# Strassen's seven products for half of a first feed-forward layer, in six of eight batches

## The chip, the cores and the metric

The kernel runs on one core of a Trainium2 chip, as a single launch. The metric is device time in microseconds (us): the median of several runs of the whole program. A core has five engines that matter here, each with its own in-order queue of instructions: TensorE (PE in the profile; its weight loads are listed apart as PEld), VectorE (DVE), ScalarE (ACT), GpSimd (POOL) and SyncE (SP), which issues most of the DMAs. Matmuls add up in PSUM, an on-chip memory of eight banks; all else lies in SBUF.

## The reference

```python
def _attn_ref(q, k, v, g_q, g_k):            # (8, 12, 448, 64): batch, heads, seq, head_dim
    q_n, k_n = rmsnorm(q, g_q), rmsnorm(k, g_k)
    scores = np.matmul(q_n, k_n.transpose(0, 1, 3, 2)) / np.sqrt(64)
    attn = np.exp(scores - scores.max(-1, keepdims=True))
    attn = attn / (attn.sum(-1, keepdims=True) + 1e-9)
    return np.matmul(attn, v)

def _moe_ref(x, w_in, w_out):                # x: (3584, 768), w_in: (768, 2048), w_out: (2048, 768)
    h = x @ w_in
    return gelu_tanh(h) @ w_out
```

The attention output of the 12 heads is laid side by side to make x (8 batches of 448 tokens, 768 columns), and x goes through two dense layers with a tanh-GELU between them. d_ff is 2048, which the kernel sees as 16 blocks of 128.

## The kernel before, in words

**Stages.** Batch after batch (loop at L1009) the kernel alternates two stages. The first-layer stage of batch b multiplies win by x of that batch and applies the GELU into the tile g. The attention stage of batch b+1 (`attention`, L584) then runs scores, exponentials, row sums and the product with v of the next batch, and fills the gaps on TensorE with the second layer (wout times g) of an earlier batch, cut into steps by the generator `quartered` (L475, one step is four matmuls; written "r" in the order string). Batch 0 has its own code. After the first layer of batch 7, `final` (L728) does the last 512 tokens of the second layer with Strassen's seven products in place of eight, in two halves of 128 tokens each.

**TensorE.** In the steady stages the 128x128 array is used as four 64x64 quadrants. The two row halves r hold two halves of the contraction, the two column halves a hold two halves of the output block. Four matmuls, one for each quadrant, run side by side; four such matmuls are called a quad below. Both row halves must add into the same PSUM bank, but not at the same time, so the work goes in two turns: in turn 0 row half r writes bank r, in turn 1 it writes bank 1-r, and `follows` (L468) makes TensorE wait for its own matmul at a change of turn. `mm1_turn` (L523) does one turn for a pair of d_ff blocks: six quads of 448 columns over the six contraction chunks c. There are eight pairs of blocks, so a first-layer stage of a batch from 1 on has 8 pairs x 2 turns x 6 chunks x 4 = 384 matmuls of 448 columns, and eight GELUs on ScalarE (L543).

**PSUM.** The eight banks are four tiles of two banks, in the list `rounds`; `pair` (L70) takes the one that is longest in use. The open second-layer tile is taken out of the list while it is filled, so the units of attention (one unit: the scores of one block of keys, "u") rotate among the other three. A unit can start only when the earlier content of its tile was read: by the exponential (L343), by a product's reader, or by an eviction of a finished second-layer tile (`evict`, L505, "E").

**Order.** The order on TensorE within a steady attention stage is written out by hand in STEADY (L571). Its first string is TensorE's: "5r u 11r uu 8r uu 8r 1r u 6r u 4r u 5r uu 6r su ..." where s is the row sums of a chunk of heads and x its product with v. Its second string is VectorE's: "A0 E0 B0 F0 G0 T0 R0 ..." where A, B, F and G add exponentials (L355 to L362), E0 evicts the first second-layer tile (L513), T, R and S make and spread reciprocals, and M writes x (`quad_x`, L418, L422). The product s of a chunk reads the result of G. What stands in the list "first" of `extra` is issued at the start of the stage, ahead of A0 on its queue.

**Side work of a first-layer stage.** A table of steps (`m1`, L1038 to L1074) issues at given places the work for later batches: GpSimd normalizes q and k of batch b+1 (L278), SyncE transposes them by DMA (L319) and loads batch b+2 (L124), ScalarE and GpSimd square them (L162, L164), VectorE sums the squares (L173) and scales kT (`gain`, L325). A 1x1 copy (`gpsimd_waits`, L874) makes GpSimd wait for VectorE.

**Batch 7.** The same table issues the sums of weights (`weight_sum`, L712, four operations of 3072 elements per partition) and of tokens (`token_sums`, L719) for the last stage.

## Time and profile before

| what | us |
|---|---|
| median of 3 runs (388.73 to 389.92) | 389.68 |
| the profiled execution's own time | 389.53 |
| its span, first to last instruction | 387.8 |
| between the two | 1.73 |
| TensorE matmul busy in the span | 379.0 |
| ScalarE busy | 276.6 |
| VectorE busy | 259.9 |
| GpSimd busy | 126.0 |

The profile is that of one execution. Its page gives busy time by engine, the chain of work that ended last, and groups of instructions with their mean duration in ns; the trace behind it answers by line, by shape and by time. Times in a timeline are us from the start of the span; an engine's next independent instruction can start a little before the one ahead is listed as ended, and a matmul's listed duration holds its way through the array, so the pace of TensorE is read from start to start.

### The profile page before, as it was taken

How to read it: one execution, taken by the hardware profiler on the slowest of the kernel's cores; microseconds unless marked ns; L12 is line 12 of the kernel's file. 1: busy time of each engine (PE TensorE's matmuls, PEld its weight loads, DVE VectorE, ACT ScalarE, POOL GpSimd, SP SyncE). 2: the span in 40 equal slices, each digit the busy share in tenths (PEclk: the TensorE clock that was granted, in tenths of full speed). 3: DMA queues.
4: the chain of work that ended last, by engine and by line, in shares of the span. 5: the costliest groups of instructions: out<-in, count | busy, mean ns of one | idle time of the engine just before them, and what ended most of it. 6: DMA issues, size and time to landing. Idle time of an engine off the chain costs nothing.

```text
span 387.8 us, 17506 instructions
## 1 busy us (share of the span) xinstructions
PE 379.0 (98%) x8020; PEld 294.2 (76%) x8020; DVE 259.9 (67%) x394; ACT 276.6 (71%) x348; POOL 126.0 (33%) x109
## 2 busy tenths in 40 slices
PE   8899999999999999999999999999999999999995
PEld 5565586679888788877888778877888778887653
DVE  5998949984896259835589156963588503895743
ACT  6995599677994689757996589946897449953400
POOL 5996504448105440083102740064400810000000
PEclk9999999999999999999999999999999999999999
DMA  8999999979914992369822995159823630220033
GB/s 274 318 232 210 210 227 230 263 176 181 222 44 99 258 199 55 85 139 224 176 73 64 181 257 110 45 111 235 111 61 82 109 59 19 69 64 5 2 79 83
DMA packets 65085, 54.66 MB, mean 141 GB/s; under 512 B 37748, under 2 KB 61172, under 8 KB 65012
## 3 DMA queue, kind: packets, MB, share of 16 engines
q1 hardware_dynamic: 54576, 41.43, 44.5%
q0 software_dynamic: 10128, 11.80, 18.4%
q8 instruction: 62, 1.02, 1.0%
q10 hardware_dynamic: 308, 0.33, 0.3%
q14 instruction: 11, 0.09, 0.1%
HBM read 45.61 MB, written 11.01 MB: 146 GB/s over the span
## 4 chain that ended last, share of the span: by engine, by line
PE 92%; ACT 5%; DMA 1%; issue 1%; DVE 0%; POOL 0%
PE t L537 33%; PE t L495 32%; PE t L387 9%; PE t L335 8%; PE t L754 5%; ACT ex L343 4%; PE t L556 4%; DMA rawq<-in_q_dram 1%; PE h L436 1%; PE tp L296 1%; PE o L387 0%; POOL nrmq L278 0%; DVE ss L173 0%; ACT sq L162 0%; PE os L387 0%
## 5 line engine op out<-in xcount | busy, mean ns | idle before, releaser
L343 ACT ACTIVATE ex<-t,shift 128x896 bf16<-128x896 f32 x168 | 156.1, 1012 | 3.0 <-PE t L335 2.6
L495 PE MATMUL t<-wout,g 64*64 64x384 bf16 (+1 forms) x3456 | 152.0, 305 | 0.0
L495 PEld LDWEIGHTS <-g 64*64 64x64 bf16 x3456 | 115.4, 107 | 17.6 <-issue 0.2
L537 PE MATMUL t<-xT,win 64*64 64x448 bf16 x2688 | 128.7, 349 | 0.0
L537 PEld LDWEIGHTS <-win 64*64 64x64 bf16 x2688 | 98.0, 107 | 29.2
L543 ACT ACTIVATE g<-t 128x896 bf16<-128x896 f32 x56 | 50.5, 915 | 56.8 <-PE t L537 56.7
L173 DVE TENSOR_REDUCE ss<-sq 128x14 f32<-128x896 f32 (+3 forms) x45 | 44.3, 998 | 49.4 <-ACT sq L162 47.0
L335 PE MATMUL t<-qT,kT 64*64 64x448 bf16 x672 | 59.9, 351 | 1.5 <-ACT ex L343 0.6
L876 POOL COPY mark<-es 1x1 bf16<-1x1 bf16 x7 | 1.2, 177 | 134.8 <-DVE es L362 126.4
L355 DVE TENSOR_TENSOR es<-ex 128x1792 bf16<-128x1792 bf16 x21 | 22.3, 1061 | 28.9 <-ACT ex L343 28.9
L278 POOL TENSOR_TENSOR nrmq<-rawq,rinv 128x896 bf16<-128x896 f32 (+1 forms) x21 | 34.8, 1658 | 19.5 <-ACT rinv L205 10.5
L278 POOL TENSOR_TENSOR nrmk<-rawk,rinv 128x896 bf16<-128x896 f32 (+1 forms) x21 | 34.6, 1647 | 0.0
L387 PE MATMUL t<-ex,vb 64*64 64x448 bf16 x588 | 32.4, 350 | 0.5 <-issue 0.5
L335 PEld LDWEIGHTS <-kT 64*64 64x64 bf16 x672 | 26.2, 106 | 8.0 <-issue 1.9
L397 DVE STREAM_TRANSPOSE st<-t 128x448 f32<-128x448 f32 x42 | 24.7, 627 | 9.6 <-PE t L387 9.6
L387 PEld LDWEIGHTS <-vb 64*64 64x64 bf16 x672 | 23.2, 107 | 8.6 <-issue 2.1
L409 DVE STREAM_TRANSPOSE rb<-rc 128x896 f32<-128x896 f32 (+1 forms) x25 | 26.7, 1068 | 0.3
L422 DVE TENSOR_TENSOR xT<-t,rb 128x896 bf16<-128x896 f32 x21 | 22.8, 1086 | 0.9 <-PE t L387 0.2
L513 ACT COPY osb<-t 128x768 f32<-128x768 f32 (+1 forms) x18 | 12.6, 701 | 14.0 <-PE t L495 14.0
L358 DVE TENSOR_TENSOR es<-es,ex 128x1792 bf16<-128x1792 bf16 x21 | 22.3, 1062 | 0.0
L164 POOL TENSOR_TENSOR sq<-rawq 128x896 f32<-128x896 f32 (+1 forms) x9 | 13.6, 1510 | 24.3 <-DVE ss L173 11.6
L325 DVE TENSOR_SCALAR kT<-kT,gcols 128x896 bf16<-128x896 bf16 x19 | 12.1, 639 | 11.2 <-DMA kT<-nrmk 11.2
(122 smaller groups left out, 322.5 us busy)
## 6 DMA issues: line engine op xcount, KB each, us to landing
rawq<-in_q_dram SPq DMA_DIRECT2D x22, 448.0 KB, 4.6
rawk<-in_k_dram SPq DMA_DIRECT2D x22, 448.0 KB, 6.3
out_dram<-osb SPq DMA_DIRECT2D x36, 192.0 KB, 2.8
vb<-in_v_dram POOLq DMA_DIRECT2D x6, 672.0 KB, 8.1
out_dram<-osb SPq DMA_DIRECT2D x38, 96.0 KB, 2.2
win<-in_moe_w_in_dram POOLq DMA_DIRECT2D x8, 384.0 KB, 10.4
wout<-in_moe_w_out_dram POOLq DMA_DIRECT2D x3, 768.0 KB, 17.2
vb<-in_v_dram POOLq DMA_DIRECT2D x2, 448.0 KB, 15.2
```

Source lines behind the costliest of these rows:

```text
L173: nc.vector.reduce_sum(sss[b][:, seat(b, c), "qk".index(n), hs, ts], squares(b, c, n, hs, ts), axis=AX.X)
L278: eng.tensor_mul(nrms[n, b, c][:, ts].rearrange("p t a d -> p a t d"), raws[n, b, c][:, :, ts], root[:, :, ts].to_broadcast([P, 2, m, D]),)
L335: nc.tensor.matmul(sc[r * R:(r + 1) * R, a, :S], kT[rs, c, t, r], qT[b][rs, c, :, r], start=True, stop=True,)
L343: nc.scalar.activation(exs[b, c][:, t], scs.pop((b, c, t))[:, :, :S], AF.Exp, scale=scale, bias=shift)
L355: nc.vector.tensor_add(es, ex[:, :2], ex[:, 2:4])
L387: nc.tensor.matmul(o[r][a * D:(a + 1) * D], vb[b % 2][rs, 2 * c + a, i] if what else ones[rs], es[i][rs, a], start=(i == 0), stop=(i == n ...
L397: nc.vector.transpose(st[:, r].rearrange("p a b -> p (a b)"), o[r])
L409: nc.vector.transpose(oas["rb"][:, rs].rearrange("p r s -> p (r s)"), rc.to_broadcast([128, (rs.stop - rs.start) * m, 32]),)
L422: nc.vector.tensor_mul(xT[b][:, 2 * c:2 * c + 2], oas["o", c, 1][:, :, :S], oas["rb"])
L495: mm = nc.tensor.matmul(o[a * R:(a + 1) * R, bank, :hi - lo], g[rs, f, at:at + R], wout[rs, f, lo:hi], start=(n == 0), stop=(n == len(step ...
L537: mm = nc.tensor.matmul(h[a * R:(a + 1) * R, j, :S], win[rs, c, at:at + R], xT[b][rs, c], start=begin and c == cs[0], stop=end and c == cs ...
L543: nc.scalar.activation(g[:, 2 * i:2 * i + 2, (b % 2) * S:(b % 2 + 1) * S], h[:, :, :S], AF.Gelu_apprx_tanh,)
```

## The change

**First layer of batches 2 to 7.** Eight of the 16 d_ff blocks (0 to 3 and 8 to 11) are computed by Strassen's seven products instead of eight. The weights are cut by d_ff (blocks 0 to 3 against 8 to 11) and by contraction (even against odd chunks); x is cut by tokens (two times 224) and by contraction. One product in one turn is `half`: 24 matmuls of 224 columns, six quads. The class `Seven` holds three PSUM tiles X, Y and Z. Products accumulate in them: X takes products 1, 6, 7 and 4 one after the other, Y takes 2, Z takes 5 and 3. In between ScalarE copies X to SBUF three times (`keep`, float32, 896 elements per partition), and VectorE adds a kept X to Y, a kept X to Z, and the other kept X to Z again (three additions of 896). Four GELUs read the results, each for four blocks and 224 tokens. The other eight blocks ("lone" pairs 2, 3, 6, 7) stay with `mm1_turn`, in parts of three chunks put between the products. `rest` is the written-out order.

**Sums.** `in_sums` makes the weight sums once: four VectorE operations on 3 x 512 bfloat16 elements per partition, put last in "first" of the attention stage of batch 2; one of them overwrites a quarter of the used part of win. `x_sums` makes four sums of 3 x 224 elements at the start of each of the six first-layer stages.

**Side work.** From batch 2 on the table has new places: the four squares of batch b+2, chunk 0, come first on ScalarE; GpSimd waits for `x_sums` between the first and the second chunk that it normalizes; one square of chunk 1 goes from ScalarE to GpSimd; loads, transposes, totals and gains have other steps.

**Memory.** x has one buffer instead of two, rb shares the buffer of st, and one weight sum of the last stage lies in two raw tiles.

**Last stage.** `weight_sum(1)` moves from the first-layer stage of batch 7 into `final`, behind the last token sums. The second row of each half is stored as whole rows, one DMA on SyncE's queue and one on ScalarE's, instead of two halves with two DMAs each on SyncE's.

```diff
-    xp = ctx.enter_context(tc.tile_pool(name="xp", bufs=2))
+    xp = ctx.enter_context(tc.tile_pool(name="xp", bufs=1))
...
-            oas["rb"] = stp.tile([128, 2, S], F32, tag="rb", name="rb")
+            oas["rb"] = stp.tile([128, 2, S], F32, tag="st", name="rb")
...
+    def in_sums():
+        a11, a21, a12, a22 = wv[:, 0, :, fs1], wv[:, 0, :, fs2], wv[:, 1, :, fs1], wv[:, 1, :, fs2]
+        nc.vector.tensor_sub(wx[:, 1], a21, a11)
+        nc.vector.tensor_add(wx[:, 0], wx[:, 1], a22)
+        nc.vector.tensor_sub(wx[:, 2], a12, wx[:, 0])
+        nc.vector.tensor_add(a21, a21, a22)
...
+        def half(self, i, name, turn, ms=range(NCH)):
...
+            if before != turn:
+                follows(mm)
...
+            for n in range(2):
+                for m in ms:
+                    for r in range(2):
+                        bank, rs = (r + turn) % 2, slice(r * D, (r + 1) * D)
+                        for a in range(2):
+                            at = (bank * 2 + n) * 128 + a * R
+                            mm = nc.tensor.matmul(
+                                t[a * R:(a + 1) * R, bank, n * QS:(n + 1) * QS],
+                                self.lhs[i][rs, m, at:at + R], self.rhs[i][rs, m],
...
+        def early(self):
+            two = range(NCH - 1)
+            for turn in range(2):
+                mm1_turn(self.b, LONE[0], turn, early, begin=not turn)
+                self.half(1, "X", turn, two)
+                self.half(2, "Y", turn, two)
+        def rest(self, steps):
...
+            self.x_sums()
+            side(0)
+            half(1, "X", 1, one)
+            mm1_turn(b, LONE[0], 1, late)
+            half(2, "Y", 1, one)
+            half(1, "X", 0, one)
+            self.keep(0)
+            mm1_turn(b, LONE[0], 0, late, end=True)
+            half(2, "Y", 0, one)
+            add(self.of("Y"), self.of("Y"), self.snaps[0])
+            self.gelu(self.of("Y"), 0, 0)
+            side(1)
+            lone(1, 0, 0, begin=True)
+            half(6, "X", 0)
+            side(2)
+            lone(1, 0, 1)
+            half(5, "Z", 0)
+            half(6, "X", 1)
+            self.keep(1)
+            side(5)
+            half(5, "Z", 1)
+            lone(1, 1, 0)
+            side(8)
+            half(7, "X", 1)
+            rounds.append(rounds.pop(0))
+            lone(2, 0, 0, begin=True)
+            half(7, "X", 0)
+            self.keep(0)
+            add(self.snaps[0], self.of("Z"), self.snaps[0])
+            lone(1, 1, 1, end=True)
+            self.gelu(self.snaps[0], 1, 1)
+            side(11)
+            lone(2, 0, 1)
+            half(4, "X", 0)
+            half(3, "Z", 1)
+            half(4, "X", 1)
+            self.gelu(self.of("X"), 1, 0)
+            side(15)
+            lone(3, 0, 0, begin=True)
+            half(3, "Z", 0)
+            add(self.of("Z"), self.of("Z"), self.snaps[1])
+            self.gelu(self.of("Z"), 0, 1)
+            side(17)
+            lone(3, 0, 1)
+            lone(2, 1, 0)
+            lone(2, 1, 1, end=True)
+            lone(3, 1, 0)
+            lone(3, 1, 1, end=True)
...
+        if b > 1:
+            sevens[b] = Seven(b)
+            sevens[b].early()
...
         token_sums(slice(NJ - 2, NJ))
+        weight_sum(1)
...
-            put_out(t, 1, last)
             add(c2[:, first], product(4, t), c2[:, first])
-            put_out(t, 1, first)
+            put_out(t, 1, slice(0, d_model), (nc.sync, nc.scalar))
...
+            extra += [("first", lambda: gain(2, 2)), ("first", in_sums)]
+        elif b + 1 < B:
+            m1 += [(0, lambda: gpsimd_waits(ess[b, NCH - 1][:1, 0, 0, :1])),
+                   (0, lambda: normed_both(b + 1, 0, nc.gpsimd)),
+                   (0, lambda: gpsimd_waits(sevens[b].xs[:1, 3, 0, :1])),
+                   (0, lambda: normed_both(b + 1, 1, nc.gpsimd)),
+                   (0, lambda: normed_both(b + 1, 2, nc.gpsimd)),
+                   (2, lambda: transposed(b + 1, 0)), (8, lambda: transposed(b + 1, 1)),
+                   (11, lambda: transposed(b + 1, 2))]
...
+                m1 += [(5, lambda n=n: total(b + 2, 0, n)) for n in "qk"]
+                m1 += [(15, lambda a=a: squared(b + 2, 1, "q", a)) for a in range(2)]
+                m1.append((15, lambda: square(b + 2, 1, "k", nc.gpsimd)))
+                m1 += [(17, lambda n=n: total(b + 2, 1, n)) for n in "qk"]
+                for n in "qk":
+                    m1.append((17, lambda n=n: square(b + 2, 2, n, nc.gpsimd)))
+                    extra.append(("first", lambda n=n: total(b + 2, 2, n)))
+            m1 += [(5, lambda: gain(b + 1, 0)), (17, lambda: gain(b + 1, 1))]
             extra.append(("first", lambda: gain(b + 1, 2)))
+        else:
+            m1 += [(5, sums_homes), (5, lambda: weight_sum(3)), (5, lambda: weight_sum(2)),
+                   (11, lambda: weight_sum(4)), (17, lambda: token_sums(slice(2, 6))),
+                   (17, lambda: token_sums(slice(0, 2)))]
```

More of the change, by code (lines that the diff above doesn't have):

```diff
@@ L568 @@
+    sevens = {}
     early, late = range(HP - 2), range(HP - 2, HP)
@@ L716, in weight_sum @@
         x, y = {3: (b12, b22), 2: (b11, sw[3]), 4: (b21, sw[2]), 1: (b12, b11)}[i]
+        if i == 4:
+            m = NJ // 2
+            for n, t in enumerate(sw[4]):
+                js = slice(n * m, (n + 1) * m)
+                nc.vector.tensor_sub(t, x[:, js], y[:, js])
+            return
         nc.vector.tensor_sub(sw[i], x, y)
@@ L1037 @@
                     (f"a{at}", lambda n=n: total(2, 0, n))]
[L1038 removed]
+        elif b == 1:
             m1.append((0, lambda: gpsimd_waits(ess[b, NCH - 1][:1, 0, 0, :1])))
[L1041 to L1055 removed]
@@ L1056 @@
-        if 0 < b and b + 2 < B:
-            m1.append((4, lambda: loads(b + 2, 1)))
-            if b > 1:
-                m1.append((8, lambda: loads(b + 2, 2)))
+            halves = [(n, slice(a, a + 1)) for n in "qk" for a in range(2)]
+            m1 += [(0, lambda n=n, hs=hs: square(2, 1, n, nc.gpsimd, hs)) for n, hs in halves]
+            m1 += [(0, lambda n=n, hs=hs: total(2, 1, n, hs)) for n, hs in halves]
+            m1 += [(0, lambda n=n: total(2, 2, n)) for n in "qk"]
+            m1.append((0, lambda: rsqrt_last(2, slice(1, NCH))))
@@ L1068 @@
-        if 0 < b and b + 1 < B:
-            extra.append(("first", lambda: gain(b + 1, 2)))
-        if b + 1 == B:
-            m1.append((4, sums_homes))
-            m1 += [(f, lambda i=i: weight_sum(i)) for f, i in ((4, 3), (6, 2), (8, 4), (10, 1))]
-            m1 += [(f, lambda js=js: token_sums(js))
-                   for f, js in ((7, slice(0, 4)), (11, slice(4, 6)))]
+                m1.append((13, lambda n=n: square(3, 2, n, nc.gpsimd)))
+                extra.append(("first", lambda n=n: total(3, 2, n)))
@@ L1075 @@
         m1 = plan(*m1)
-        for f in range(nf // 2 if b == 0 else nf):
+        if b > 1:
+            sevens[b].rest(m1)
+        for f in range((nf // 2, nf)[b] if b < 2 else 0):
             i, part = f // 4 * 2, f % 4
```

116 lines of the change are left out of this document (87 added, 29 removed).

## The prediction, made before the changed kernel was run

> **What bounds the kernel now.** I read the page's busy shares first, then the chain of work that ended last, then who waited on TensorE, then the timelines of one first-layer stage and of the start of one attention stage.
>
> ```profile
> span 387.8 us, 17506 instructions
> PE 379.0 (98%) x8020; PEld 294.2 (76%) x8020; DVE 259.9 (67%) x394; ACT 276.6 (71%) x348; POOL 126.0 (33%) x109
> ...
> PE 92%; ACT 5%; DMA 1%; issue 1%; DVE 0%; POOL 0%
> ```
>
> TensorE is the bound: it carries 92% of the chain. In its waits the longest total is 0.8 us, at the start (L1133 is the launch); behind it comes one of 0.6 us:
>
> ```profile
> PE o L269 <- PEq L1133: 0.8, 1, 0.8
> PE t L335 <- ACT ex L343: 0.6, 2, 0.3
> ```
>
> So from batch 1 on nothing holds TensorE up. A matmul less is time less, and a wait added to TensorE is time more, since no later wait is there to absorb it. The rest is a balance of the two.
>
> **Matmuls saved.** The chain shows a whole first-layer stage, and stretches of second-layer matmuls that are only 192 columns wide:
>
> ```profile
> 211.07 18.16 PE t L537 x384
> ...
> 249.78 2.13 PE t L495 x84
> ...
> 253.24 0.91 PE t L495 x44
> ```
>
> A stage is 96 quads of 448 columns in 18.16 us: 0.189 us a quad. Eleven quads of 192 columns (the last row) take 0.91 us: 0.083. On the line through the two, a quad of 224 columns takes 0.096 us. The eight blocks cost 48 quads of 448 now, 9.08 us; the seven products cost 7 x 2 turns x 6 = 84 quads of 224, 8.06 us. That is 1.02 us less in each of six stages, 6.1 us in all, if nothing waits. A stage would last 17.14 us.
>
> Here the Trainium skill speaks against the change. Its page "TensorE: Matmul & The Clock Gate", section "Wait — 56ns, not 53.3ns?", has starts of matmuls never closer than about 25 ns. By it a quad would last 0.100 us and the stage 17.5 us, 0.34 us of the 1.02 us lost. The eleven quads of 192 run at 0.91/44 = 20.7 ns a matmul, below that floor, so I go by the row; but that burst is short, and the rivals return to it.
>
> **Waits added within a stage.** Products that add in one tile X are separated by a copy to SBUF on ScalarE, and Z by an addition on VectorE. Prices, from the groups by shape (the copy of 896 elements is extended from 384 and 768, the addition of 896, from PSUM and SBUF, is taken as the like product that writes x):
>
> ```profile
> L543 ACT ACTIVATE g<-t 128x896 bf16<-128x896 f32 x56 | 50.5, 915 | 56.8 <-PE t L537 56.7
> ...
> L422 DVE TENSOR_TENSOR xT<-t,rb 128x896 bf16<-128x896 f32 x21 | 22.8, 1086 | 0.9 <-PE t L387 0.2
> ...
> L513 ACT COPY osb<-t 128x768 f32<-128x768 f32 x12 | 9.7, 812 | 0.0
> ...
> L513 ACT COPY osb<-t 128x384 f32<-128x384 f32 x6 | 2.9, 478 | 14.0 <-PE t L495 14.0
> ```
>
> The copy: 0.812 + 128 x (0.812 - 0.478)/384 = 0.92 us. The addition: 1.09 us. Then the lags between engines, from three timelines: TensorE to ScalarE, ScalarE to VectorE and TensorE to VectorE.
>
> ```profile
> 210.87 0.95 PE L537 MATMUL t<-xT,win 64*64 64x448 bf16 x16
> ```
> ```profile
> 215.28 1.73 ACT L543 ACTIVATE g<-t 128x896 bf16<-128x896 f32 x2 [3.14 <-PE t L537]
> ```
> ```profile
> 364.81 0.92 ACT L543 ACTIVATE g<-t 128x896 bf16<-128x896 f32 x1 [0.22 <-PE t L537]
> 365.76 0.42 DVE L723 TENSOR_TENSOR vb<-g 128x512 bf16<-128x512 bf16 x1 [1.66 <-ACT g L543]
> ...
> 371.21 1.46 PE L754 MATMUL t<-tw,vb 128*128 128x384 bf16 x8
> ...
> 371.41 0.56 DVE L771 TENSOR_TENSOR osb<-t,osb 128x384 f32<-128x384 f32 x1 [0.67 <-PE t L754]
> ```
>
> The first pair of blocks is done after 22 quads, 4.16 us behind 210.87, at 215.03; its GELU starts at 215.28: 0.25 us. A GELU that ends at 365.73 starts VectorE at 365.76: 0.03. A product that gives way to the next at 371.21 starts VectorE at 371.41: 0.20. From ScalarE or VectorE back to TensorE I take 0.05 (a row for it comes below).
>
> Now the written order. Between the last matmul of `half(7, X, 0)` and the first of `half(3, Z, 1)` TensorE has two lone parts of three quads (0.567 each) and `half(4, X, 0)` (0.575): 1.71 us of work. `half(3, Z, 1)` must wait until the addition has read Z, and the addition until the copy is made: 0.25 + 0.92 + 0.03 + 1.09 + 0.05 = 2.34 us. TensorE stands for 0.63 us. Three times a copy of X alone stands between (in front of `half(6, X, 0)`, `half(7, X, 1)` and `half(4, X, 0)`): 0.25 + 0.92 + 0.05 = 1.22 against 1.14 us of other work, 0.08 each; the third lies within the 0.63. Sum 0.79 us a stage: the stage lasts 17.9 us, and six stages give 6 x (18.16 - 17.93) = 1.4 us, not 6.1. Bounds: nothing waited, 6.1; copy and addition 0.1 us longer each, 0.5 us less a stage, 1.6 us worse than before in all. I take 1.4, since each term has a row.
>
> What is queued behind TensorE's wait for Z is the rest of the stage. What else lies on the other queues is free at the time:
>
> ```profile
> 210.86 1.28 ACT L675 ACT_TABLE_LOAD   x1
> ```
> ```profile
> 212.27 1.09 DVE L422 TENSOR_TENSOR xT<-t,rb 128x896 bf16<-128x896 f32 x1
> ```
> ```profile
> 212.64 1.68 POOL L278 TENSOR_TENSOR nrmk<-rawk,rinv 128x896 bf16<-128x896 f32 x1
> ```
> ```profile
> L162 ACT ACTIVATE sq<-rawq 128x448 f32<-128x448 f32 x22 | 11.9, 570 | 0.4 <-DMA rawq<-in_q_dram 0.4
> ```
>
> The four squares ahead of the first copy (0.57 us each) fill ScalarE's hole behind the table load, from 212.14 to 214.4; that copy is due 4.25 us behind the stage's start, at 215.1. `x_sums` follows VectorE's x at 213.36. Its four sums are 672 elements each; the row of 512 above took 0.42, so I take 0.5. It is needed 5.2 us behind the start, at 216.1, by its second sum; even if GpSimd's operation held it up until 214.32 it would be in time. GpSimd's new wait for `x_sums` costs it 1 to 2 us (214.32 to about 216); behind it lie two chunks to normalize, and on SyncE's queue their transposes and the loads of batch b+2, all wanted only at steps 15 and 17 or in the next attention stage. The two totals (1.08 each) and the gain (0.44) at step 5, from 217.2, end before the late addition at 222.5. At the end, the addition on Z and two GELUs (1.09, 0.9, 0.9) fit beside the last five parts (2.84 us), so the last GELU starts as late behind the last matmul as now, and the exponentials too.
>
> **The weight sums.** They are issued once, on VectorE, ahead of A0 in the attention stage of batch 2. That stage before, VectorE and then TensorE:
>
> ```profile
> 99.55 0.44 DVE L325 TENSOR_SCALAR kT<-kT,gcols 128x896 bf16<-128x896 bf16 x1
> 100.25 1.09 DVE L355 TENSOR_TENSOR es<-ex 128x1792 bf16<-128x1792 bf16 x1 [0.27 <-ACT ex L343]
> 101.26 0.95 DVE L513 COPY osb<-t 128x768 f32<-128x768 f32 x1
> ...
> 103.97 0.63 DVE L362 TENSOR_TENSOR es<-es,ex 128x896 bf16<-128x896 bf16 x1
> ```
> ```profile
> 102.27 0.47 PE L335 MATMUL t<-qT,kT 64*64 64x448 bf16 x4
> ...
> 104.65 0.45 PE L387 MATMUL t<-es,ones 64*64 64x448 bf16 x4
> ```
>
> E0 empties the PSUM tile at 102.21, and the unit that takes this tile, the eighth (u7), starts at 102.27; G0 ends at 104.60 and the row sums s0 that read it start at 104.65. This is the lag of 0.05, and it says that VectorE has no slack here at all: A0 later by so much is TensorE later by so much. In front of A0 VectorE is idle for 0.27 us only. The price of the four sums lies between two rows:
>
> ```profile
> L717 DVE TENSOR_TENSOR tw<-wout,tw 128x3072 bf16<-128x3072 bf16 x2 | 3.5, 1755 | 0.0
> ...
> L724 DVE TENSOR_TENSOR kT<-vb,g 128x1024 bf16<-128x1024 bf16 x1 | 0.7, 693 | 0.0
> ```
>
> 1536 elements: 0.69 + 512 x 1.06/2048 = 0.96 us; where the next does not need the one before, it starts 0.08 early, as 101.26 against 100.25 + 1.09 shows; four of them 3.6 us. A0 starts 3.6 - 0.27 = 3.3 us late, and u7 with it. Behind u7 everything on TensorE queues, and no wait further on gives it back. Bounds: 0.57 ns an element, as the longer row has it, gives 3.5 - 0.27 = 3.2 and with all overlap 3.0; 0.68, as the shorter, gives 3.9. I take 3.3.
>
> **The rest.** `weight_sum(1)` (1.75 us) in `final` ends some 6 us behind the first-layer stage and is needed by the seventh product of 1.30 us, at 7.8; the PSUM tile that it keeps the addition of the second product from emptying is needed at 6.5, so nothing, or 0.3 us if I am that far out. rb in st's buffer, and x in one: their users follow each other on VectorE or lie a stage apart; nothing.
>
> At the very end SyncE's issues are the queue:
>
> ```profile
> 382.39 1.11 SPq L456 DMA_DIRECT2D out_dram<-osb  x2
> ...
> 384.44 0.56 SPq L456 DMA_DIRECT2D out_dram<-osb  x1
> ```
> ```profile
> out_dram<-osb SPq DMA_DIRECT2D x36, 192.0 KB, 2.8
> ...
> out_dram<-osb SPq DMA_DIRECT2D x38, 96.0 KB, 2.2
> ```
>
> With two issues less the last one goes out at about 383.55 instead of 384.44; but twice 192 KB now leave at 382.4 at once, and what used to leave from 381.1 is late by 1.3 us. Between -0.9 and +0.4 I take -0.3.
>
> Sum against the profiled run's own 389.53: -1.4 + 3.3 - 0.3 = +1.6, so **391.1 us**; the median of the runs shown is 389.68, 0.15 above that run, which is within what I can tell.
>
> **Rivals.**
>
> *The waits for X and Z are hidden.* If TensorE were let into Z before copy and addition are both through, most of the 6.1 us comes: at best 389.5 - 6.1 + 3.3 - 0.3 = 386.4. Against it stands a row for each term. 5%.
>
> *The weight sums are hidden,* because A0 is late for other reasons, or u7's tile is free before: 389.5 - 1.4 - 0.3 = 387.8. Against it: 0.27 us of idle and 0.06 between E0 and u7. 8%.
>
> *VectorE is late for A0 in the later stages too* (slower). In the following stages A0 still has room:
>
> ```profile
> 230.23 1.08 DVE L173 TENSOR_REDUCE ss<-sq 128x14 f32<-128x896 f32 x1 [0.58 <-POOL sq L164]
> 231.24 0.44 DVE L325 TENSOR_SCALAR kT<-kT,gcols 128x896 bf16<-128x896 bf16 x1
> 235.24 1.09 DVE L355 TENSOR_TENSOR es<-ex 128x1792 bf16<-128x1792 bf16 x1 [3.56 <-ACT ex L343]
> ```
>
> This one A0 waited 3.56 us for its exponentials. GpSimd's last squares, which the totals ahead of A0 need, start only when VectorE has freed their buffers, behind the addition on Z: I make them end some 1.7 us later than now, and a gain caught behind a GpSimd operation can add 1.6 us, as this one shows, beside which GpSimd was running:
>
> ```profile
> 308.03 2.01 DVE L325 TENSOR_SCALAR kT<-kT,gcols 128x896 bf16<-128x896 bf16 x1 [4.13 <-DMA kT<-nrmk]
> ```
> ```profile
> 308.11 1.68 POOL L278 TENSOR_TENSOR nrmq<-rawq,rinv 128x896 bf16<-128x896 f32 x1
> ```
>
> It decides from 3.56 us on; each microsecond beyond, in four stages, is 4 us. With half a microsecond to one: 393 to 395. 17%.
>
> *Matmuls of 224 columns can't be issued at that pace for long* (slower). They must start every 24 ns, in parts of 24. The longest fast stretch of the rows above is the 84 matmuls in 2.13 us (five quads of 384 columns and 16 of 192), 25.4 ns each. If that is the limit, 336 matmuls a stage lose 336 x 1.4 ns = 0.47 us, six stages 2.8 us: 393.9. Against it: the 44 at 20.7 ns, and the pace of the whole stage, 528 matmuls in 17.1 us, 32 ns each. 8%. By the 25 ns of the skill's rule above it would be 6 x 0.34 = 2.0 us, 393.1.
>
> *The clock drops.* The wait at u7 leaves TensorE idle for 3.3 us. Every slice of the page shows nine tenths or more, with no idle stretch of that length to read from:
>
> ```profile
> PEclk9999999999999999999999999999999999999999
> ```
>
> If the clock came back at half for as long as the wait, the kernel would lose 3.3/2 us more: 392.8. 5%. The same page of the Trainium skill (section "What's actually happening") says that one idle window of about 3.4 us, free-running, halves the clock; 3.3 us would just not fill one, and no run here shows it.
>
> **How the numbers follow.** The forecast has 57%; its own range is 390.0 to 392.3, from the bounds of the Z wait (half of them on each side) and the tail. The two faster rivals have 13%, the three slower ones 30%. About 0.3% (1.2 us) is what a measurement of this kernel can tell from no change. The lower 40% of the forecast, 23%, lies within it of 389.68, with 1% more for half-hidden sums: faster 12%, same 24%, slower 64%. The range of eight in ten leaves out the fully hidden waits, half of the hidden sums and the dearer half of the VectorE rival: 388.2 to 394.0.
>
> **What would show it.** Right: in the profile after, 17.9 us for a first-layer stage, with a TensorE wait of 0.6 us on the addition's line in each of six stages and about 0.1 on the copy's; one wait of about 3.3 us at L335 for E0's copy in the stage of batch 2; A0 elsewhere still waiting for the exponentials. Wrong: first-layer matmuls of 224 columns at more than 0.1 us a quad; TensorE waits at other attention stages; a granted clock below 1; no TensorE wait at u7.

## The result and the profile after

| | before | changed kernel |
|---|---|---|
| median, us | 389.21 (388.55 to 389.92, 4 runs) | 399.11 (396.4 to 400.26, 4 runs) |
| ratio | | 1.0239 [1.0208, 1.027] |
| the profiled execution's own time | 389.53 | 396.4 |
| its span | 387.8 | 394.6 |

The changed kernel is slower: by 2.4% in the ratio above, by 9.9 us between the medians. Forecast were 391.1 us and a range up to 394.0; the side was right, the size was not. A second series of the same kernel (r_after, below) gave 398.33. The profiled execution, at 396.4, is the fastest of its four; what the others had on top is taken up with the clock.

The first and second part of the page of the changed kernel, and its chain by engine:

```profile
span 394.6 us, 19289 instructions
PE 376.3 (95%) x8884; PEld 301.5 (76%) x8884; DVE 299.2 (76%) x441; ACT 290.2 (74%) x358; POOL 134.3 (34%) x118
...
PE 79%; DVE 8%; ACT 6%; issue 2%; DMA 2%; POOL 1%; SPq 1%; DVEq 0%; ACTq 0%; POOLq 0%
```

TensorE is busy for 2.7 us less than before (376.3 against 379.0), but the span is 6.8 us longer: 9.5 us more in which it stands. Its instructions are 864 matmuls and 864 weight loads more. Its waits, longest total first:

```profile
PE t L537 <- issue: 3.8, 3, 1.7
PE t L335 <- DVE osb L513: 2.6, 1, 2.6
PE t L627 <- DVE xs L696: 1.8, 5, 0.4
PE t L627 <- issue: 1.0, 1, 1.0
```

Two of the four are the prediction's own: u7 behind E0 (L513), and product 3 behind the addition on Z (L696). The other two are "issue": time in which TensorE waited for nothing that the profile names, in the middle of a first-layer stage. The chain of waits says where. A stage runs from its first L537 to the first L495 behind it:

```profile
123.87 0.76 PE t L537 x16
...
138.95 2.27 PE t L537 x47
141.22 1.67 issue
...
143.80 0.81 PE t L495 x20
...
170.66 0.76 PE t L537 x16
171.42 0.77 PE t L627 x32
172.19 0.76 PE t L537 x16
172.94 0.96 PE t L627 x40
177.00 1.73 PE t L627 x72
...
181.17 0.92 ACT xs L641
182.11 1.10 DVE xs L696
183.26 1.34 PE t L627 x48
...
188.63 0.81 PE t L495 x20
...
215.64 0.76 PE t L537 x16
...
227.74 1.04 issue
...
233.25 1.72 issue
...
236.27 0.80 PE t L495 x17
...
263.17 0.76 PE t L537 x16
...
281.90 0.81 PE t L495 x20
...
308.86 0.76 PE t L537 x16
...
326.78 0.81 PE t L495 x20
```

The stages of batches 2 to 6 last 19.93, 17.97, 20.63, 18.73 and 17.92 us, and that of batch 7, read the same way, 17.97. Where nothing is called "issue", a stage has the 17.93 us that were forecast. In the stages of batches 2, 4 and 5 it is 2.0, 2.7 and 0.8 us longer: 5.5 us in all, 4.8 of them listed as idle on issue. The attention stage of batch 2 is the other loss; VectorE there, and TensorE's unit u7:

```profile
99.41 0.95 DVE L577 TENSOR_TENSOR wx<-win 128x1536 bf16<-128x1536 bf16 x1
...
102.26 0.95 DVE L580 TENSOR_TENSOR win<-win 128x1536 bf16<-128x1536 bf16 x1
103.13 1.08 DVE L355 TENSOR_TENSOR es<-ex 128x1792 bf16<-128x1792 bf16 x1
104.13 0.95 DVE L513 COPY osb<-t 128x768 f32<-128x768 f32 x1
```
```profile
105.13 0.38 PE L335 MATMUL t<-qT,kT 64*64 64x448 bf16 x4 [2.64 <-DVE osb L513]
```

The four sums, 0.95 us each as forecast, put A0 from 100.25 to 103.13 and u7 from 102.27 to 105.13. So the 6.8 us by which the span grew are: 2.8 in the attention stage of batch 2, 5.5 in the stages with idle on issue, less 1.3 for six stages (6 x 18.16 - 6 x 17.95), less about 0.2 in the later attention stages and at the end.

### The profile page after: what moved, and what is told of

It reads as the page before. It is cut to its first block, busy times and chain, and to the rows that moved or that the text cites. A ratio compares the mean times of both kernels' runs of the same rounds, so it can differ in the third digit from the quotient of the medians.

```text
span 394.6 us, 19289 instructions
## 1 busy us (share of the span) xinstructions
PE 376.3 (95%) x8884; PEld 301.5 (76%) x8884; DVE 299.2 (76%) x441; ACT 290.2 (74%) x358; POOL 134.3 (34%) x118
## 3 DMA queue, kind: packets, MB, share of 16 engines
q8 instruction: 69, 1.13, 1.2%
## 4 chain that ended last, share of the span: by engine, by line
PE 79%; DVE 8%; ACT 6%; issue 2%; DMA 2%; POOL 1%; SPq 1%; DVEq 0%; ACTq 0%; POOLq 0%
PE t L495 29%; PE t L537 13%; PE t L627 12%; PE t L387 8%; PE t L335 7%; PE t L920 5%; ACT ex L343 4%; PE t L556 4%; DVE ss L173 2%; DMA kT<-nrmk 2%; DVE xs L696 1%; ACT xs L641 1%; DMA rawq<-in_q_dram 1%; POOL nrmq L278 1%; DVE st L397 1%
## 5 line engine op out<-in xcount | busy, mean ns | idle before, releaser
L495 PE MATMUL t<-wout,g 64*64 64x384 bf16 (+1 forms) x3456 | 153.1, 305 | 0.0
L495 PEld LDWEIGHTS <-g 64*64 64x64 bf16 x3456 | 117.5, 107 | 16.8 <-issue 0.5
L537 PE MATMUL t<-xT,win 64*64 64x448 bf16 x1536 | 87.3, 349 | 3.9 <-issue 3.8
L537 PEld LDWEIGHTS <-win 64*64 64x64 bf16 x1536 | 54.7, 107 | 15.1 <-issue 5.7
L335 PE MATMUL t<-qT,kT 64*64 64x448 bf16 x672 | 61.0, 351 | 4.0 <-DVE osb L513 2.6
L173 DVE TENSOR_REDUCE ss<-sq 128x14 f32<-128x896 f32 (+3 forms) x45 | 43.4, 994 | 8.0 <-ACT sq L162 5.6
L543 ACT ACTIVATE g<-t 128x896 bf16<-128x896 f32 x32 | 29.2, 917 | 9.5 <-PE t L537 9.4
L627 PEld LDWEIGHTS <-win 64*64 64x64 bf16 x1152 | 31.5, 107 | 5.4 <-issue 2.5
L641 ACT COPY xs<-t 128x896 f32<-128x896 f32 x18 | 16.3, 907 | 26.1 <-PE t L627 22.5
L335 PEld LDWEIGHTS <-kT 64*64 64x64 bf16 x672 | 27.4, 106 | 10.7 <-issue 4.3
L387 PE MATMUL t<-ex,vb 64*64 64x448 bf16 x588 | 32.4, 350 | 0.2 <-issue 0.2
L387 PEld LDWEIGHTS <-vb 64*64 64x64 bf16 x672 | 22.7, 107 | 8.9 <-issue 1.6
L627 PEld LDWEIGHTS <-wx 64*64 64x64 bf16 x864 | 23.3, 106 | 6.0 <-issue 2.9
L645 ACT ACTIVATE g<-t 128x896 bf16<-128x896 f32 x18 | 16.5, 917 | 10.7 <-DVE t L708 5.1
```

The costliest lines, as they stand in the source:

```text
L173: nc.vector.reduce_sum(sss[b][:, seat(b, c), "qk".index(n), hs, ts], squares(b, c, n, hs, ts), axis=AX.X)
L335: nc.tensor.matmul(sc[r * R:(r + 1) * R, a, :S], kT[rs, c, t, r], qT[b][rs, c, :, r], start=True, stop=True,)
L387: nc.tensor.matmul(o[r][a * D:(a + 1) * D], vb[b % 2][rs, 2 * c + a, i] if what else ones[rs], es[i][rs, a], start=(i == 0), stop=(i == n ...
L495: mm = nc.tensor.matmul(o[a * R:(a + 1) * R, bank, :hi - lo], g[rs, f, at:at + R], wout[rs, f, lo:hi], start=(n == 0), stop=(n == len(step ...
L537: mm = nc.tensor.matmul(h[a * R:(a + 1) * R, j, :S], win[rs, c, at:at + R], xT[b][rs, c], start=begin and c == cs[0], stop=end and c == cs ...
L543: nc.scalar.activation(g[:, 2 * i:2 * i + 2, (b % 2) * S:(b % 2 + 1) * S], h[:, :, :S], AF.Gelu_apprx_tanh,)
```

## The experiments

The question was what the idle on issue is. **Theory:** TensorE's instructions come from memory by DMA in blocks of 16 KB, and a block comes late where the loads of q and k fill the DMA engines; the change raises a stage from 768 instructions (384 matmuls, as many weight loads) to 1056, so blocks are used up faster. **Rival 1:** matmuls of 224 columns in quadrants can't be issued at that pace, loads or not. **Rival 2:** it is a wait for X, Y or Z that the profile doesn't name.

**The same matmuls on the whole array (e1_full).** One matmul of 128x128 weights instead of four of 64x64, in the seven products alone:

```diff
-                    for r in range(2):
-                        bank, rs = (r + turn) % 2, slice(r * D, (r + 1) * D)
-                        for a in range(2):
-                            at = (bank * 2 + n) * 128 + a * R
-                            mm = nc.tensor.matmul(
-                                t[a * R:(a + 1) * R, bank, n * QS:(n + 1) * QS],
-                                self.lhs[i][rs, m, at:at + R], self.rhs[i][rs, m],
...
+                    at = (turn * 2 + n) * 128
+                    nc.tensor.matmul(
+                        t[:, turn, n * QS:(n + 1) * QS],
+                        self.lhs[i][:, m, at:at + 128], self.rhs[i][:, m],
```

> The changed kernel, but the seven products use the whole 128x128 array: 84 matmuls of 224 columns a stage in place of 336, of the same 0.096 us each as a quad; all else stays. TensorE then has 552 matmuls' instructions in a first-layer stage, not 1056 counted with the weight loads' pairs but half of that. Theory 'fetch' (TensorE runs out of instructions, since a block of 16 KB lasts 4.2 us in the new stages and its DMA is late among the loads): the idle times put down to 'issue' in the stages of batches 2, 4 and 5 go, about 5 us, and the stage lasts 17.9 us everywhere; 391 to 392 us. Rival 'own waits' (the idle comes from something in the order of the products, such as a wait that the profile does not name): the idle stays, 396 to 399 us.

Measured: 403.48 us (402.27 to 404.1, 4 runs) against 389.45, ratio 1.0345 [1.0309, 1.038]. The idle on issue within the stages is gone, but every stage now lasts about 19.8 us. The chain of its second such stage, to be laid beside the four lines from 170.66 above:

```profile
171.99 0.76 PE t L537 x16
172.75 0.87 PE t L621 x8
173.62 0.88 PE t L537 x16
174.50 1.06 PE t L621 x10
```

The same work takes 0.87 instead of 0.77, 0.88 instead of 0.76, 1.06 instead of 0.96: each change between quadrants and whole array costs 0.10 to 0.12 us, and a stage has some twenty. The Trainium skill has this in "TensorEngine Tiling (Array Packing)", section "Key Properties": a change of tiling mode drains TensorE. The run thus fits the theory on the idle, but its time, far from the 391 to 392 of that theory, measures something else.

**No loads in those stages (e2_noloads).** The loads of chunks 1 and 2 of q and k are left out in the first-layer stages of batches 2 to 5 and chunk 0's data used again, so the outputs of those chunks are another's:

```diff
-                m1 += [(2, lambda: loads(b + 2, 1)), (8, lambda: loads(b + 2, 2))]
+                for n in "qk":
+                    for c in (1, 2):
+                        raws[n, b + 2, c] = raws[n, b + 2, 0]
```

> The changed kernel without the loads of q and k, chunks 1 and 2, in the first-layer stages of batches 2 to 5 (batches 4 to 7 use chunk 0's data again: this part of the computation is left out). TensorE's instructions are unchanged. Theory 'fetch', if the lateness of the blocks comes from the loads' traffic: no idle 'issue' over 0.3 us, 391 to 393 us. If the number of instructions alone is too much for the fetch: idle stays as in the changed kernel, 396 to 399 us. Rival 'own waits': the same 396 to 399.

Measured: 391.85 us (389.89 to 392.83, 10 runs) against 389.45, ratio 1.0053 [1.0029, 1.0077]. All six stages last 17.9 us, and no wait on issue is left in them; TensorE's two longest are

```profile
PE t L335 <- DVE osb L513: 2.6, 1, 2.6
PE t L627 <- DVE xs L696: 2.1, 6, 0.4
```

With the loads gone, some 7 us of the 9.9 are gone (by medians; the profiled run, with 5.5 us of idle, was the fastest of the changed kernel), and the matmuls are issued at the forecast pace. Rivals 1 and 2 both fall as causes by themselves.

**The count of instructions without Strassen (e3_split).** The kernel before, with the matmuls of eight blocks of batches 2 to 7 each cut into two of 224 columns: 576 matmuls a stage, no copies, no sums.

```diff
+            parts = (0, S // 2, S) if b > 1 and i in (0, 1, 4, 5) else (0, S)
+            for lo, hi in zip(parts, parts[1:]):
...
-                            h[a * R:(a + 1) * R, j, :S], win[rs, c, at:at + R], xT[b][rs, c],
+                            h[a * R:(a + 1) * R, j, lo:hi], win[rs, c, at:at + R],
+                            xT[b][rs, c, lo:hi],
```

> The kernel before, with no Strassen, but the matmuls of eight d_ff blocks in batches 2 to 7 cut in two of 224 columns: 576 matmuls a stage in place of 384, the same sums, the same order and waits. By the pace of a quad (0.096 against 0.189) a stage grows by 0.13 us, all by 0.8 us: 390. Theory 'fetch': TensorE idles on 'issue' in some of the stages that load, 2 to 5 us in all: 392 to 395. Rival 'own waits': no such idle, 390.

Measured: 400.49 us (400.26 to 405.27, 4 runs) against 389.45, ratio 1.0301 [1.0236, 1.0366]. A cut that changes no dependence costs as much as the whole change (11.0 us against 9.9 between the medians, with intervals that overlap), and more than the 392 to 395 that the theory gave. The chain of its first such stage:

```profile
120.33 11.53 PE t L539 x387
131.87 1.30 issue
133.17 4.10 PE t L539 x128
137.27 1.82 issue
139.09 3.18 PE t L539 x61
```

Here one sees the block. Between two idles lie 128 matmuls, in this stage and in the three that follow; with their weight loads that is 256 instructions. The changed kernel shows the same: from 228.78 to 233.25 its timeline holds 128 matmuls. And the size fits the row of the instruction queue in the changed kernel's profile, 69 transfers with 1.13 MB, 16 KB each: 64 bytes an instruction. The row follows TensorE's count from kernel to kernel: 62 transfers with the 8020 matmuls before, 69 with 8884, 48 with the 6184 of e6. The idle is 9.3 us in eight places (L539 on issue), none in the stages of batches 6 and 7, which load nothing. The Trainium skill, "Runtime: NRT & Kernel Launch", section "Instruction fetch mechanics", has the blocks of 16 KiB, 256 instructions, and calls the cost of passing from one to the next mostly hidden. The size agrees; that it is hidden does not, by 1.3 and 1.8 us here.

**The same cut without the loads (e8_split_noloads).** The edit of e3, and the loads left out as in e2 (the same chunks' outputs are another's):

```diff
-            m1.append((4, lambda: loads(b + 2, 1)))
...
+                for n in "qk":
+                    for c in (1, 2):
+                        raws[n, b + 2, c] = raws[n, b + 2, 0]
```

> The kernel before with the matmuls of eight d_ff blocks of each first-layer stage of batches 2 to 7 cut into two of 224 columns, and without the loads of chunks 1 and 2 of q and k in those stages of batches 2 to 5 (the data of chunk 0 is used again, so the output for those chunks is another). Theory (TensorE's instructions, fetched in blocks of 16 KB, come late where those loads fill the DMA queues): no stage idles more than 0.3 us on issue, and the time is 388 to 392 us where the same cut with its loads took 400.5. Rival (the number of instructions alone is more than TensorE can be given, loads or not): the idle of some 1.3 to 1.8 us a block stays, and the time is 398 to 402.

Measured: 390.52 us (390.27 to 391.49, 10 runs) against 389.62, ratio 1.0024 [1.0002, 1.0046], and in the chain each of its six stages is one piece, without an idle:

```profile
122.38 18.28 PE t L539 x576
```

So count alone isn't it (18.28 against 18.16), and loads alone aren't either, since the kernel before has them: it is both. The DMA queues of the changed kernel in its first Strassen stage (123.9 to 143.8), then in that of batch 6 (308.9 to 326.8), which transposes but loads no q and k:

```profile
q1 hardware_dynamic: 7056, 3.84, 98.2%
q8 instruction: 3, 0.05, 1.0%
```
```profile
q1 hardware_dynamic: 5728, 1.57, 61.9%
q8 instruction: 4, 0.07, 1.5%
```

The columns are packets, MB and share of the 16 engines. The instruction blocks are 1% of the load beside 98% of other traffic. The kernel before has nearly as full a stage (92.9%), but a block of 128 matmuls lasts it 128/384 x 18.16 = 6.1 us, and the new one 128/528 x 17.95 = 4.4.

The trace holds each transfer of the instruction queue, and so it shows the late blocks themselves. In the changed kernel's profile there are four such idles. Their transfers began at 140.44, 226.46, 232.57 and 275.55, landed 0.93 to 1.03 us later, and TensorE went on 1.3 to 1.5 us behind each landing, every time 88 to 91 matmuls past a multiple of 128. The eight idles of e3 end likewise, 1.2 to 1.5 us behind a landing. The transfers are not slow: the median of all 69 is 0.98 us. They start late. Counted from the step of TensorE into the block before (the matmul 128 earlier), those four began after 2.7 to 4.0 us, with the DMA engines full all that time; in the stage of batch 6 none began later than 0.6 us. The idle at 233.25 is one such sum: 3.8 us to the start, 0.9 for the transfer and 1.5 behind it make 6.2 us, for a block that lasts 4.5.

**Strassen from batch 3 only (e4_from3).** Batch 2 keeps its first layer as before, and the weight sums go into that stage.

```diff
-            extra += [("first", lambda: gain(2, 2)), ("first", in_sums)]
+            extra += [("first", lambda: gain(2, 2))]
+        elif b == 2:
...
+            m1 += [(9, lambda: gain(b + 1, 0)), (10, in_sums), (14, lambda: gain(b + 1, 1)),
+                   (15, last_sum)]
```

> The changed kernel, but Strassen from batch 3 on only, and the weight sums in the first-layer stage of batch 2, where VectorE has idle time: three of them at step 10, the one that overwrites win at step 15. The wait of 2.9 us at the eighth unit goes, and batch 2's own 0.2 us of gain and its idle with it. Profiled run 391 to 394 by what is left of the idle. Theory 'clock' (the spread of the changed kernel's runs, 396.4 to 400.3 at a granted clock of 0.999 to 0.991, is the clock dropping behind the 2.9 us wait): all runs at 0.998 or more and within 1.5 us of each other. Rival: the drop follows the idle on 'issue', then clocks of 0.991 to 0.996 stay.

Measured: 391.7 us (390.16 to 396.52, 10 runs) against 389.45, ratio 1.0055 [1.0028, 1.0082]. The wait at u7 is gone and the clock is 0.997 or more in every run. Leaving out the longest run, 396.52, the other nine still spread by 3.7 us, where I had expected 1.5; idle on issue is still there in the profiled one (1.2 and 0.4 us), and how late a block comes need not be the same in each run, though only one was profiled.

**The changed kernel again (r_after).** No edit.

> The changed kernel again, unaltered, beside its variants on the same chip. By the theory as it stands (a wait of 2.9 us for the weight sums, 3 to 7 us of TensorE idle on 'issue' in stages that load, 1.7 us more when the clock comes back at half behind the first wait, and 0.2 us gained in each stage) it takes 396 to 401 us, with a median near 399, and runs with a granted clock of 0.995 or less are the slower ones.

Measured: 398.33 us (396.89 to 399.66, 4 runs) against 389.02, ratio 1.0236 [1.0197, 1.0275]. The wait at u7 was 3.42 us in this profile, the idle on issue at L537 4.6.

**Another order in the last third (e5_order).** A lone part goes ahead of product 3, so that more work stands between the reads of Z:

```diff
+            side(15)
+            lone(2, 1, 0)
             half(3, "Z", 1)
             half(4, "X", 1)
             self.gelu(self.of("X"), 1, 0)
-            side(15)
-            lone(3, 0, 0, begin=True)
...
+            lone(3, 0, 0, begin=True)
             lone(3, 0, 1)
-            lone(2, 1, 0)
```

> The changed kernel with another order in the last third of the stage: a lone part stands between half(4, X, 0) and half(3, Z, 1), half(4, X, 1) and half(3, Z, 0) follow at once, and the squares of step 15 come before the GELU of X. TensorE then has 2.28 us of work against 2.34 us of copy and addition. Theory 'Z wait': stages without idle on 'issue' last 17.3 to 17.4 us and not 17.95, TensorE's waits for L696 are under 0.1 each; 3 to 3.5 us less than the changed kernel in the sum of six stages. Rival: the wait returns elsewhere (the later GELU of Z holds up the next stage), stages at 17.9.

Measured: 395.56 us (393.41 to 396.23, 4 runs) against 389.02, ratio 1.0147 [1.0106, 1.0187]. The waits on L696 are gone; the stages without idle last 17.4 us instead of 17.95 (171.58 to 189.00 in the chain), close to the 17.14 that were worked out for no wait at all. The idle on issue stays, 3.9 us at L537 and 0.5 at L627.

**All first-layer matmuls on the whole array (e6_allfull).** Strassen from batch 3 and the weight sums in the stage of batch 2, as in e4, with e5's order and with the matmuls of the lone blocks, and of batches 1 and 2, written as e1's: no change between quadrants and whole array within a stage, and 132 matmuls in it instead of 528.

```diff
+            at = (2 * i + turn) * 128
+            nc.tensor.matmul(
+                h[:, turn, :S], win[:, c, at:at + 128], xT[b][:, c],
+                start=c == 0, stop=c == HP - 1,
+            )
```

> Strassen from batch 3 with the weight sums in the stage of batch 2, the other order, and all matmuls of the first-layer stages on the whole 128x128 array: 84 of 224 and 48 of 448 columns a stage, a quarter of the instructions, and no change between quadrants and whole array within a stage. Theory 'fetch' with 'switch' (a change between the two ways costs 0.12 us, as 12 quads of 448 in 0.69 for 0.567 us beside whole-array products show): no idle on 'issue', stages of 17.3 to 17.6 us in batches 3 to 7, no wait at the eighth unit, clock 0.998 or more: 385 to 387 us. Rival 'whole array is slower by itself': stages over 18.2, no gain over before.

Measured: **387.72 us** (387.12 to 388.48, 9 runs) against 389.02, ratio 0.9965 [0.9953, 0.9977]. It is faster than both kernels, than the one before by 0.35%. Its first Strassen stage:

```profile
167.79 0.86 PE t L530 x4
...
182.29 2.84 PE t L530 x15
185.13 0.94 PE t L495 x20
```

17.34 us, loads and all, without idle on issue.

**The whole array without Strassen (e7_before_full).** The kernel before with e6's edit of `mm1_turn` alone, batches 1 to 7.

> The kernel before, without Strassen, with the first-layer stages of batches 1 to 7 on the whole array: 96 matmuls of 448 columns a stage. It tells how much of the run before this one is Strassen's. Theory 'switch': 18.2 to 18.4 us a stage, the same time as before within 1.5 us, 388 to 391. If fewer instructions alone gain: under 388.

Measured: 391.12 us (390.43 to 392.45, 6 runs) against 389.02, ratio 1.005 [1.0027, 1.0072]; a stage 18.26 us instead of 18.16. Seven such stages make 0.7 of the 2.1 us; where the rest goes was not followed up. So the whole array is no gain by itself, and e6's gain is Strassen's.

**The weight sums elsewhere (e9_sums_first).** The changed kernel, with the four sums ahead of the gain of chunk 1, where VectorE stood waiting for kT:

```diff
-            extra += [("first", lambda: gain(2, 2)), ("first", in_sums)]
+            extra += [("first", lambda: gain(2, 2))]
+            extra.insert(0, ("first", in_sums))
```

> The changed kernel with the four weight sums moved on VectorE's queue alone: ahead of the gain of chunk 1 in the attention stage of batch 2, where VectorE stood for 2.63 us waiting for kT (from 93.3 to 95.9), and no longer between the last gain and A0. Theory (the sums hold A0 and E0 back, TensorE waits at the eighth unit, and the clock drops behind that wait in most runs): four sums of 0.96 us end near 97.1 instead of 103.2, A0 is at most 0.5 us late, the wait at L335 for E0 falls from 2.6 us to 0.5 or less, and the granted clock is 0.998 or more in runs without a long idle on issue; 394 to 396 us where the changed kernel took 398.3 to 399.1. Rival (TensorE would wait at that unit for another reason): the wait stays over 1.5 us and the time over 397. The idle on issue in the first-layer stages stays either way, 3 to 5 us.

Measured: 394.67 us (393.96 to 395.35, 6 runs) against 389.48, ratio 1.0131 [1.0104, 1.0158]: 4 us off, in the interval of the theory. But the wait at u7 fell only to 1.78 us, not to 0.5: past the 1.5 set for the rival, though the time is not past its 397. VectorE and GpSimd show why:

```profile
92.86 2.16 DVE L577 TENSOR_TENSOR wx<-win 128x1536 bf16<-128x1536 bf16 x1
95.05 2.41 DVE L578 TENSOR_TENSOR wx<-wx,win 128x1536 bf16<-128x1536 bf16 x1
```
```profile
92.53 1.67 POOL L164 TENSOR_TENSOR sq<-rawq 128x896 f32<-128x896 f32 x1
94.97 1.68 POOL L164 TENSOR_TENSOR sq<-rawk 128x896 f32<-128x896 f32 x1 [0.77 <-DMA rawk<-in_k_dram]
```

Each of the first two sums ran into a GpSimd operation and took 1.2 and 1.45 us more; the last one ended at 99.3 instead of the 97.1 expected. From there VectorE works without a gap up to A0, which starts 1.70 us later than before (101.95 against 100.25), and u7 starts 1.69 us later (103.96 against 102.27). So what is left of the wait is the sums' too. The granted clock was 0.997 or more in all six runs.

**All of it (e10_full_sums_first).** e6 from batch 2 on, with the sums where e9 has them:

```diff
-        elif b == 2:
...
-            extra.append(("first", lambda: gain(b + 1, 2)))
+            extra.insert(0, ("first", lambda: (in_sums(), last_sum())))
...
-        if b > 2:
+        if b > 1:
```

> The changed kernel (Strassen in batches 2 to 7) with all first-layer matmuls of batches 1 to 7 on the whole array, the order of the last third turned, and the weight sums ahead of the gain of chunk 1 as in the run beside it. If fetch, waits on X and Z, and the sums are all there was, six stages of 17.35 us stand against 18.16, 4.9 us less, less 0.1 for the stage of batch 1 and up to 0.5 at the eighth unit: 384.5 to 387.5 us, up to 1 us less than the version that begins at batch 3 (387.7). Rival (the late gain of chunk 1 or the stage of batch 2 without its own side work gives the gain back): 388 or more.

Measured: **387.26 us** (386.63 to 388.16, 7 runs) against 389.48, ratio 0.9941 [0.9917, 0.9964]. Five of its stages last 17.33 us and that of batch 7 17.7; a wait of 1.1 us at u7 is left. It beats the kernel before; that it beats e6 is not settled, since the two didn't run side by side and their intervals overlap.

**The clock.** In e2's profiled run, stretches of the time behind the wait at u7, and the middle one of the changed kernel's profiled run (after the busy times: granted clock, DMA share, GB/s):

```profile
106.00:108.00 2.00, 2.00 (x28) 1.39 (x27) 1.86 (x3) 1.01 (x1) 0.00 (x0) 0.50 0.51 117
```
```profile
106.00:108.00 2.00, 2.00 (x53) 1.50 (x48) 1.33 (x3) 2.00 (x3) 0.00 (x0) 1.00 0.76 197
```

28 matmuls at half clock against 53 at full. The same dip, 3.41 us long, follows that wait in the profiles of r_after, e1_full and e5_order, where it comes once more behind an idle of 2.0 us on issue. So it comes in some runs and not in others, behind much the same wait: 2.64 us without a dip, 2.65 with one. The times go with it: the changed kernel ran 396.4 at a mean clock of 0.999, and 398.61 to 400.26 at 0.991 to 0.995; e2 389.89 to 390.97 at 0.998 or 0.999, and 391.68 to 392.83 at 0.993 to 0.995. That is about 2 us a dip, a little over half of 3.41, and most of what lies between the profiled 396.4 and the median. With the wait gone (e4) or at 1.78 and less (e9, e10), no run was below 0.997. (0.997 alone is no dip: the clock also halves behind the last matmuls, in e6's profile from 383.06 on.)

What decides was not tried by a run, but the traces tell. From the clock's first rise on, all its changes in a profile lie whole multiples of 3.413 us apart; in e5 the two dips start at 105.02 and 234.72, 38 of them. Laid on this grid, each of the five dips ahead of the last matmuls follows a step of the grid in which TensorE was idle for 2.0 to 2.8 us. No step with less is followed by one in any of the 13 profiles, not even e3's with 1.82. In the changed kernel's profile the grid cut the wait of 2.64 us into 1.48 and 1.16; in e2's, 2.26 of the 2.65 fell into one step. So it is luck where the wait falls on the grid, and that differs from run to run. The Trainium skill's rule that was weighed in the prediction, one free-running idle window of about 3.4 us ("TensorE: Matmul & The Clock Gate", section "What's actually happening"), has the length and the free running as they are here; but the window need not be idle as a whole, since 2.0 us in it were enough.

## Why the prediction was wrong, point by point

- **TensorE is the bound, and a wait added is time more:** right. Both losses of the profiled run went through to the end in full.
- **Matmuls saved:** the pace was right, 0.096 us a quad (1.73 us for 18 at 177.00), and e6 and e10 last 17.3 us a stage with no waits to speak of. The condition "if nothing waits" was the failed step. I counted waits on ScalarE and VectorE and took TensorE's own instructions as always there. A stage went from 768 to 1056 of them, blocks of 256 came late among the loads, and this cost 5.5 us in the profiled run. e2, e3 and e8 show it from three sides, and the transfers of the blocks show it directly. The profile before had a sign of it that I passed over: TensorE's waits list 0.5 us on issue at L387, an idle that ends 1.6 us behind the landing of a block.
- **Waits added within a stage:** right. Copy 0.92, addition 1.10, stage 17.92 to 17.97 where undisturbed, forecast 17.93. The wait named on L696 is 0.4 and not 0.6, because the waits view counts from a matmul's modelled end (0.36 us); from start to start the gap is 0.61. e5, where the wait is gone, has stages 0.5 us shorter.
- **The weight sums:** right in the mechanism. Forecast 3.3 us at u7; 2.64 and 3.42 in two profiles. In the first, the stage's end moved by 2.8, under the lower bound of 3.0: the four sums took 3.72 us (99.41 to 103.13), but VectorE came to them at 99.41, where before it was busy until 99.99.
- **The end:** forecast -0.3; from the first product of `final` to the end of the span 23.0 us against 23.0 before, so nothing. `weight_sum(1)` cost nothing, as forecast.
- **Rivals:** VectorE late for A0 in later stages (17%) did not happen; TensorE has no such wait. "Can't be issued at that pace for long" (8%, 393.9) named the place and had another cause and a price half as large: it is not the pace of matmuls but of fetching them, and only while loads run. The dropping clock (5%) came in most runs, about 2 us, priced at 1.65; the chance was too low, and in which runs it came was luck. Forecast and rivals were treated as alternatives, but they came together: the forecast's +1.6, 5.5 for the fetch and about 2 for the clock make 9.1 of the 9.9, and the range had no room for that.

What stays open: what holds back the start of a block's transfer. That it queues behind the packets of the loads on the same engines fits the traces, but is argued and not shown; a transfer that has begun is not slow. The stage of batch 3 had no idle in the profiled run because its late block (begun 3.2 us after the step at 185.03) was wanted only in the attention stage behind it, at 190.40, and had landed at 189.13.

## What to carry to other kernels

When a change cuts matmuls into smaller ones, count TensorE's instructions as a resource: instructions per us, against the 256 of a block, in the stages where the DMA engines are full. By the sum for the idle at 233.25, a block had to last some 6 us there, which is an estimate. A full-array matmul does the work of four quadrants in the same time with a quarter of the instructions, but only if its neighbours use the whole array too. Before putting one-off work on a queue, look for a hole that the engine has anyway, and at what GpSimd does in that hole.

## What the runs showed of the hardware

- TensorE stood for up to 2.0 us for a block of 256 instructions, in stages of 1056 and 1152 TensorE instructions that load q and k, though not in every one of these; in such stages without those loads (e2, e8, batches 6 and 7) it did not.
- A block's transfer of 16 KB took about 1 us (median 0.98). It began up to 0.6 us behind TensorE's step into the block before where no loads of q and k ran (batch 6), and 2.7 to 4.0 us behind it at the four idles among the loads; TensorE went on 1.3 to 1.5 us behind the landing.
- A change between 64x64 quadrants and the whole array took 0.10 to 0.12 us on TensorE.
- A VectorE operation on two inputs in SBUF, 0.95 us alone, took 2.16 and 2.41 us beside a GpSimd operation of 1.7 us. The Trainium skill, "SBUF — State Buffer", section "SBUF: two separate sides", has such a VectorE operation blocked for as long as a GpSimd operation holds the ports that they share; the sums agree, 1.2 and 1.45 us late.
- The clock changed only on a grid of 3.413 us. A step of that grid with 2.0 us or more of TensorE idle was followed by 3.41 us at half clock; one with less (1.8 in e3) was not.
